# A one-core attention and mixing block: more idle products on TensorE, some of them into other PSUM sums, and a new instruction order

## The chip, the core and the metric

The kernel runs on one core of a Trainium2 chip. The metric is the device time of one execution in microseconds (us). Three executions of the kernel before took 656.92, 652.56 and 657.92 us, median 656.92. A core has TensorE (PE, with its weight loads PEld), VectorE (DVE), ScalarE (ACT), GpSimd (POOL) and SyncE (SP), which issues the DMAs; each runs its own instruction list strictly in the order in which the program gives it. A wait at the head of a list therefore holds everything behind it on that engine.

## The reference

```python
def _attn_ref(q, k, v, s):                       # q, k, v: (4, 8, 576, 64); s: (4, 8, 576)
    scores = scale * np.matmul(q, k.transpose(0, 1, 3, 2))
    cum = np.cumsum(np.maximum(s, 0.0), axis=-1)
    bias = -(cum[:, :, :, None] - cum[:, :, None, :])
    scores = np.where(causal, -1000000000.0, scores + np.minimum(bias, 0.0))
    attn = np.exp(scores - np.max(scores, axis=-1, keepdims=True))
    attn = attn / (np.sum(attn, axis=-1, keepdims=True) + 1e-09)
    return np.matmul(attn, v)
# x = heads side by side: (4, 576, 512)
#   h = relu(x^T @ w_tok1) @ w_tok2;  u = x + h^T;  u = u + relu(u @ w_ch1) @ w_ch2
#   out = (sigmoid(causal 5-tap convolution of u) * (u @ w_val)) @ w_out
```

## The kernel before

**Work.** The four batches run one behind the other, each in four pairs of heads. A pair `b_hp` loads q, k and v, scales and splits them, and goes through five query tiles i = 0 to 4: `score` (PE writes a PSUM bank `S`, DVE masks it into `x` with a running minimum), `expo` (ACT), the transposed probabilities, then `av` (PE multiplies them with v). All `av` products of a pair land in one PSUM bank, `xbank`: tiles 0 to 2 first, then `norm` and `x_value` read that bank (DVE, or DVE and ACT) and write `x32`, and only then may tiles 3 and 4 write the same columns. The four pairs of the first batch are "wide": their probabilities are transposed on PE (`p_turn`: tiles `p` and `pb`, copied out by ACT) and multiplied in 32-bit form. The later pairs split the probabilities in two 16-bit halves (`p_split`, tile `p`) and transpose them by DMA. Behind the pairs of a batch come token mixing (`t`), channel mixing (`c`, on `u` and `hT`), gate, `v` and `o`.

**Weights.** In the first 160 us the weights are decoded too. Each chunk of a weight is loaded (`raw`), unpacked by ACT and DVE into `arena`, and summed on PE: `dec.summed` adds products of a matrix of ones with the chunk to an open PSUM sum `ws_<name>`, in four steps of 128 columns for most chunks. The largest sum gives the weight's scale, by which ACT, POOL and DVE split it (`arena<-arena`).

**Order.** `ORDER` is a list of some 3,450 steps that a search wrote out: a letter for the engine (P, A, V, G, S) and a task's number. `Plan.run` takes the steps one by one and emits what they say; a replay of planned durations runs beside it. It decides one thing only: before each PE step `keep_warm` compares the planned time with how busy PE was planned to be, and where the share is under `WARM_FILL` it calls `plan.idle()`, which emits one product that nobody needs (an "idle product") so that the TensorE clock stays up. These products stand in PE's list for good. In the kernel before each writes columns 400 to 511 of `xbank` from a matrix of ones (line 530); there are 452. Because they write the bank that `norm` and `x_value` read, an idle product that stands behind those reads waits for them, and a read that stands behind an idle product waits for it.

Of the kernel before, what the change touches and what calls it, by code (L numbers as in the profile page):

```python
# [53 lines left out]
WARM_FROM, WARM_FILL, GAP1 = 12e3, 0.75, 13.87  # L54
# [27 lines left out]
S10 S0 V0 S7 P8 S12 A11 P1 V1 V1 A11 V11 P1 V1 V11 V1 P11 A9 A13 G4 A13 V13 V13 P13 S138 G6 S139 A9 G5 A3 G6 G6 S18  # L82
G6 A3 A2 V2 A2 G5 A141 A141 A141 S21 V9 V9 P9 V2 S2 S27 S32 V14 V14 A17 G17 P19 A20 A15 S140 S30 S191 V3 P142 V142
V142 P142 V142 V142 V142 A143 V143 A144 V144 S145 A20 V20 P28 A31 A31 V20 P20 S34 S145 V31 V31 P31 A33 A33 V33 V33
P33 G146 G16 S190 A22 A22 V22 V22 S46 P22 S41 S192 S44 A29 A29 V29 V29 V23 V23 G25 G25 G26 G16 A35 A35 V35 P29 S48
P149 P147 V147 A148 P155 V155 A156 P153 V153 A154 P169 V169 A170 V35 P157 A157 P175 V175 A193 S242 P171 V149 A150
P178 V178 P176 A193 P157 A157 A193 V171 A172 P179 V179 P161 P151 A151 V161 A162 P194 P159 V176 A177 V194 P157 A157
V194 P194 P173 A173 P35 V159 A160 A180 V194 V194 V194 V195 V195 G196 V196 S197 G24 S55 S197 V36 V36 V37 G37 S244
P152 G15 P42 P152 P158 P158 P163 A163 P173 A173 P163 A163 P181 A43 P173 P163 A163 P164 P164 V165 V165 V166 G167 A173
A45 A181 P181 A45 V45 A181 P181 P174 P174 V45 P45 A47 A43 V43 A181 P182 P182 S243 A47 V47 A49 V47 P47 A49 V49 A49  # L90
P168 A168 G167 V43 P43 V183 V183 V184 A185 G198 P199 P201 P211 P207 P230 P205 V199 P213 A200 V201 P221 A202 V211
P203 A212 V207 P227 A208 V230 A203 V213 A214 G49 P49 A245 S58 G185 P187 G24 P187 P215 V227 G39 V205 V221 P231 S69
S62 P223 A187 P228 P186 V40 G38 V187 P188 A245 S60 A215 P188 G188 A245 A206 V231 P246 V50 V228 P215 V50 P209 V246
P204 P204 V246 P246 V223 S294 V246 A222 V246 G39 V246 V248 V248 G247 V247 S249 S249 G250 G54 G54 A186 V189 V189 V189
G51 G51 P56 A209 P209 A215 A209 P209 A224 P225 A209 P210 A232 S296 A229 P215 A215 A59 P210 P233 A233 P216 P216 V217
V217 V218 G219 G219 A225 P225 A59 V59 V59 A57 A225 P233 A233 P225 A225 A57 V57 V57 P70 A71 P233 A233 A71 V71 V71
P226 P226 P234 P234 S295 P220 P57 A63 A63 V63 V235 A61 V63 V235 P71 S72 A61 A220 V61 A236 G237 G237 P251 V251 A252
P257 V257 A258 P265 V265 A266 P282 G53 P259 V259 A260 P59 P253 V253 A254 A297 A297 V61 P279 V279 P275 V275 G52 P273
P255 A255 V282 V273 P261 P61 S467 P63 V64 G40 P283 P263 A297 P298 V298 V298 G38 S74 A261 A73 P261 A261 V263 P298
V298 V298 V298 G300 S76 P280 A73 V283 V280 A264 A276 A274 V300 S468 P239 P239 A299 V299 S301 P267 A267 G302 A281  # L100
P261 A261 P267 P256 P256 P262 A239 P277 A267 A75 P267 P262 A277 P238 V64 G66 G66 G65 G68 A77 V73 V73 P73 S78 A267
S301 V239 P277 A75 V75 P268 P268 V269 V269 V75 A277 P277 A284 S469 P285 A238 V270 A77 A285 V77 P240 P240 G240 V241
V241 V241 G271 G271 P75 S80 P285 A470 A277 P278 P278 S525 A77 P272 A285 P285 A79 A79 V79 A272 P303 V303 P309 V309
A285 P327 V327 P317 P305 V305 P325 V79 V325 P311 V311 A470 G67 A310 G77 P77 S82 P286 G65 V317 A470 P471 V471 A304
P315 A328 G67 A306 P331 P307 V315 V471 V331 P286 V287 P471 V471 A81 V287 P334 G53 A326 A81 V81 A318 A312 P313 A307
A83 V288 G289 G289 V471 V81 P79 S84 V471 G473 P332 V332 P308 A313 A83 V83 A472 V472 P308 P81 S86 V473 S474 S474 P290
A290 A316 G52 G475 P329 V83 P313 A313 V334 A329 P291 P319 P313 A313 A319 P291 A291 V291 P329 P335 V335 P319 A85 A85
V85 P292 P292 G292 A319 P319 V85 G476 A329 P314 P314 V293 P83 S88 A333 A87 V293 V293 A319 P320 P320 V321 A87 A336
P337 A337 P337 A337 P85 S90 V87 V321 P329 V87 P87 P337 P477 P479 P484 V322 P491 G476 V323 V323 A329 P330 P330 P493
V479 P486 S92 V484 G68 S526 V477 A337 P338 P338 V491 P512 P509 A480 G476 S476 V482 V482 A478 V493 A89 G481 G481 S481  # L110
A485 V486 P502 G488 G488 A89 V89 V89 P89 A492 V339 V339 A91 A91 V91 S482 V509 A487 A340 G341 S108 V91 P504 A93 V341
S488 G489 G489 S527 P510 V510 A93 V93 S489 A528 P343 A494 A528 P343 A343 P324 V93 P93 V504 A108 A108 V343 P91 V94
G495 G495 V502 V94 V94 A324 A108 V108 P483 P483 S109 P342 A342 A503 P344 P344 A344 V345 A528 P529 V529 A95 G496 S495
V345 P110 G496 S496 V529 G506 G506 V345 P529 V512 A511 V346 S114 A515 P490 S506 V108 S112 P490 P346 V346 A111 V529
V346 A111 V111 A505 P346 V346 P513 G95 V529 V111 V529 G515 S515 A507 G507 A348 A350 V350 A349 V349 A530 V530 A531
# [346 lines left out]
def gated_block_kernel(  # L462
# [15 lines left out]
    nc = tc.nc  # L478
# [1301 lines left out]
```

## Time and profile before

| | us |
|---|---|
| median of three executions | 656.92 |
| the profiled execution | 659.9 |
| its span, first to last instruction | 658.1 |
| busy in the span: PE | 617.2 (94%) |
| DVE | 488.6 (74%) |
| ACT | 384.4 (58%) |
| POOL | 254.8 (39%) |
| mean granted TensorE clock | 0.979 |

The clock is a share of full speed: 1.00 is 2.4 GHz, 0.50 is 1.2 GHz, and those are its two levels; a figure between them is a mean over a stretch that has both. Busy PE is not PE at its peak, since a product lasts longer at the lower clock and the ends of products are modelled.

### The profile page before, as it was taken

Reading aid. Unit: us, or ns where it says so; the run is one execution under the profiler, and the core shown is the slowest. Engines: PE = TensorE matmul, PEld = TensorE weight load, DVE = VectorE, ACT = ScalarE, POOL = GpSimd, SP = SyncE. Lnnn points to the kernel's source line nnn. Section 1 sums busy time; section 2 is a strip of 40 time slices with the busy share of each in tenths; the row PEclk is TensorE's granted clock in tenths of the full one; section 3 lists DMA queues with packets and bytes.
Section 4 is the critical chain, followed back from the end, with each engine's and each line's share of the span. In section 5 each row is a group of like instructions: output and inputs, shape, how many; then the busy total and the mean of one; then the engine's idle time right before and its main releaser. Section 6 shows DMA issues by size and latency. Waiting matters only on the chain.

```text
span 658.1 us, 15930 instructions
## 1 busy us (share of the span) xinstructions
PE 617.2 (94%) x6059; PEld 498.4 (76%) x6059; DVE 488.6 (74%) x1380; ACT 384.4 (58%) x816; POOL 254.8 (39%) x367
## 2 busy tenths in 40 slices
PE   2899999969999979989998999999999999999997
PEld 2788888867778858767787887777877887678864
DVE  6888588887979968768687877877798943445672
ACT  5688498776768667645584655446576602204324
POOL 2457468343643432413454455713553210314000
PEclk9999599988999989999999999999999999999999
DMA  8986577686765828663747365844654400000002
GB/s 232 236 230 192 121 175 190 173 182 143 184 109 98 162 61 147 131 124 92 116 94 130 80 132 110 162 97 95 126 119 68 92 1 1 33 1 1 17 33 80
DMA packets 190806, 75.17 MB, mean 114 GB/s; under 512 B 178213, under 2 KB 181381, under 8 KB 190730
## 3 DMA queue, kind: packets, MB, share of 16 engines
q1 hardware_dynamic: 190730, 74.16, 51.3%
q8 instruction: 47, 0.77, 0.5%
q14 instruction: 29, 0.24, 0.1%
HBM read 33.89 MB, written 4.83 MB: 59 GB/s over the span
## 4 chain that ended last, share of the span: by engine, by line
PE 52%; DMA 4%; DVE 1%; ACT 1%; SPq 0%; issue 0%; POOL 0%; DVEq 0%; POOLq 0%; ACTq 0%
PE c L257 29%; PE o L257 7%; PE v L257 6%; PE t L257 3%; DMA pT<-p 3%; PE S L257 3%; PE xbank L257 3%; DMA qkT<-qk 1%; PE xT L257 1%; PE xm L257 1%; SPq L257 0%; DMA qk<-qkT 0%; ACT x L257 0%; DVE x L257 0%; DVE qk L257 0%
## 5 line engine op out<-in xcount | busy, mean ns | idle before, releaser
L257 PEld LDWEIGHTS <-arena 128*128 128x128 f16 x3168 | 288.9, 99 | 73.3 <-issue 4.1
L257 PE MATMUL c<-hT,arena 128*128 128x256 f16 (+1 forms) x1152 | 160.2, 287 | 3.6 <-DVE st L257 3.6
L257 PE MATMUL c<-u,arena 128*128 128x256 f16 (+1 forms) x1152 | 158.0, 288 | 0.0
L257 ACT ACTIVATE x<-x,st 128x448 f32<-128x448 f32 (+4 forms) x160 | 85.8, 556 | 56.9 <-DVE st L257 50.2
L257 POOL TENSOR_TENSOR p<-x,p 128x64 f16<-128x64 f32 (+4 forms) x83 | 68.7, 830 | 95.2 <-ACT p L257 72.1
L257 DVE CUSTOM_DVE_ANT_0 x<-S,mask,sc 128x64 f32<-128x64 f32 (+4 forms) x160 | 73.8, 485 | 25.1 <-PE S L257 13.5
L257 ACT ACTIVATE hT<-c 128x320 f16<-128x320 f32 (+1 forms) x96 | 36.3, 406 | 67.5 <-PE c L257 67.4
L257 PE MATMUL xbank<-v,pT 128*128 128x65 f16 (+1 forms) x880 | 64.9, 213 | 4.4 <-DMA pT<-p 3.3
L257 DVE SCALAR_TENSOR_TENSOR hT<-c,hT 128x320 f16<-128x320 f32 (+1 forms) x96 | 41.5, 449 | 27.8 <-ACT hT L257 27.6
L257 DVE SCALAR_TENSOR_TENSOR gate<-R,cwt,gate 128x320 f32<-128x320 f32 (+1 forms) x112 | 61.1, 564 | 1.2
L257 PE MATMUL S<-qk 67*128 67x288 f16 (+4 forms) x192 | 50.4, 285 | 4.1 <-DMA qk<-qkT 4.1
L257 PE MATMUL v<-x,arena 128*128 128x256 f16 (+1 forms) x384 | 53.9, 286 | 0.2 <-DVE x L257 0.2
L257 PE MATMUL S<-qkT 128*128 128x288 f16 (+4 forms) x192 | 50.5, 285 | 0.9 <-DVE st L257 0.9
L257 POOL TENSOR_SCALAR p<-x 128x192 f16<-128x192 f32 (+4 forms) x48 | 24.2, 505 | 61.5 <-ACT x L257 27.0
L257 PEld LDWEIGHTS <-pT 128*128 128x128 f16 x960 | 38.7, 98 | 9.4 <-DMA pT<-p 3.8
L257 PE MATMUL o<-arena,g 128*128 128x512 f16 x192 | 45.1, 379 | 0.0
L530 PE MATMUL xbank<-ones 128*128 128x112 bf16 x452 | 36.0, 228 | 6.4 <-DVE sums L257 2.9
L530 PEld LDWEIGHTS <-ones 128*128 128x128 bf16 x452 | 31.6, 108 | 9.4 <-issue 7.3
L257 ACT ACTIVATE gate<-gate 128x1280 f32<-128x1280 f32 (+1 forms) x24 | 27.9, 1162 | 14.4 <-DVE gate L257 14.0
L257 PEld LDWEIGHTS <-g 128*128 128x128 f16 x192 | 18.4, 98 | 18.1
L257 ACT ACTIVATE p<-x 128x576 f16<-128x576 f32 (+4 forms) x59 | 27.8, 477 | 5.8 <-DMA pT<-p 2.6
L257 DVE SCALAR_TENSOR_TENSOR qk<-stg,sg,qk 128x576 f16<-128x576 f32 x30 | 30.0, 1028 | 0.6 <-ACT qk L257 0.5
(209 smaller groups left out, 1090.6 us busy)
## 6 DMA issues: line engine op xcount, KB each, us to landing
raw<-in_moe_w_ch_dram SPq DMA_DIRECT2D x24, 512.0 KB, 4.6
stg<-in_q_dram SPq DMA_DIRECT2D x16, 288.0 KB, 3.3
stg<-in_k_dram SPq DMA_DIRECT2D x16, 288.0 KB, 5.3
qk<-qkT SPq DMA_DIRECT2D x32, 144.0 KB, 2.5
out_dram<-ot SPq DMA_DIRECT2D x16, 256.0 KB, 2.0
vst<-in_v_dram SPq DMA_DIRECT2D x24, 128.0 KB, 3.6
raw<-in_moe_w_val_dram SPq DMA_DIRECT2D x4, 512.0 KB
raw<-in_moe_w_out_dram SPq DMA_DIRECT2D x4, 512.0 KB
```

The lines of the kernel that those rows point to most:

```text
L257: return f(*a, **k)
L530: plan.idle = lambda: nc.tensor.matmul(xbank[:, 400:512], lhsT=ones, rhs=ones[:, 0:112], start=True, stop=True)
```

## The change

The share up to which PE is filled rises from 0.75 to 0.9. The idle product gets two forms. While nobody reads `xbank` (`read_x` is empty) it is as before. From the moment at which a `norm` has been emitted until the next `av` of tile 0 or 3 has been, it goes instead into the sum of a weight that is still open (`sums_w`): ones times columns of `mask` that hold zeros, added to that sum. If no weight's sum is open either, nothing is emitted, though the plan counts the time as filled. `ORDER` is a new list throughout; one line of each stands for it here.

```diff
-WARM_FROM, WARM_FILL, GAP1 = 12e3, 0.75, 13.87
+WARM_FROM, WARM_FILL, GAP1 = 12e3, 0.9, 13.87
...
-S10 S0 V0 S7 P8 S12 A11 P1 V1 V1 A11 V11 P1 V1 V11 V1 P11 A9 A13 G4 A13 V13 V13 P13 S138 G6 S139 A9 G5 A3 G6 G6 S18
...
+S0 V0 S7 S10 S12 S138 S139 S18 G4 P8 P1 V1 V1 P1 V1 V1 A11 A11 V11 V11 A13 G5 A13 V13 P11 A3 S21 G6 A3 V13 P13 A9 A2
...
     xbank = psX.tile([P, 512], F32, tag="X", name="xbank")
-    plan.idle = lambda: nc.tensor.matmul(xbank[:, 400:512], lhsT=ones, rhs=ones[:, 0:112], start=True, stop=True)
+    read_x, sums_w = [], []
+
+    def idle():
+        if not read_x:
+            nc.tensor.matmul(xbank[:, 400:512], lhsT=ones, rhs=ones[:, 0:112], start=True, stop=True)
+        elif sums_w:
+
+            ps, n = sums_w[-1]
+            for _ in range(max(1, 112 // n)):
+                nc.tensor.matmul(ps, lhsT=ones, rhs=mask[:, 0:n], start=False, stop=False)
+
+    plan.idle = idle
...
                 total = sum(ch[3] for ch in self.ch) * self.cw // self.nsum
+                if self.summed:
+                    sums_w.remove((self.ps, self.nsum))
                 for f in range(0, n, self.nsum):
...
                     self.summed += 1
+                if self.summed < total:
+                    sums_w.append((self.ps, self.nsum))
...
             if i in (0, 3):
                 yield PE, "X"
+                read_x.clear()
...
             xa = self.st["xa", h][:, 0:6 * DV].rearrange("p (i h d) -> p i h d", h=2, d=DV)
+            read_x.append(self)
```

The program holds 498 idle products after the change: 377 into `xbank` (line 534) and 121 into a weight's sum (line 539: 26 in `ws_c12`, 74 in `ws_c2`, 21 in `ws_wv`), against 452 into `xbank`. Ahead of the first score of the kernel there are 176 where there were 141.

PE's list in pair 0_1 (second pair of the first batch), from the last `av` of tile 2 to the first of tile 3, before; line 530 is the idle product, seven of them in the first gap, two in each of the two others:

```order
L257 MATMUL xbank_81<-v16_1_131,pT_0_1_2_1_1095 128x65 x2
L257 MATMUL xbank_81<-v16_1_131,pg_2_126 128x65
L257 MATMUL pb_0_1_3_0_1121<-ident_90,x_2_3_951 128x128 x3
L257 MATMUL pb_0_1_4_0_1132<-ident_90,x_2_4_946 128x128 x4
L530 LDWEIGHTS ones_79
L530 MATMUL xbank_81<-ones_79 128x112
...
L257 MATMUL pb_0_1_3_1_1146<-ident_90,x_3_3_1020 128x128 x3
...
L257 MATMUL pb_0_1_4_1_1160<-ident_90,x_3_4_892 128x128 x4
...
L257 MATMUL xbank_81<-v16_1_131,pT_0_1_3_0_1130 128x65 x3
```

The same place after the change:

```order
L256 MATMUL xbank_81<-v16_1_131,pT_0_1_2_1_1110 128x65 x2
L256 MATMUL xbank_81<-v16_1_131,pg_2_126 128x65
L256 MATMUL p0_0_1_4_1142<-ident_90,x_2_4_932 64x128
L256 MATMUL p0_0_1_4_1142<-ident_90,x_3_4_1004 64x128
L256 MATMUL pb_0_1_3_0_1154<-ident_90,x_2_3_963 128x128 x3
L256 MATMUL pb_0_1_4_0_1160<-ident_90,x_2_4_932 128x128 x4
L256 MATMUL pb_0_1_3_1_1165<-ident_90,x_3_3_1062 128x128 x3
L256 MATMUL pb_0_1_4_1_1173<-ident_90,x_3_4_1004 128x128 x4
L256 MATMUL xbank_81<-v16_1_131,pT_0_1_3_0_1158 128x65 x3
```

No idle product stands between tile 2 and tile 3 any more, and no weight's sum is open there: 16 transposes are all that PE has.

DVE's list at the same place, from the split of q and k (`qk16`) of the next pair to the value read (`x32<-xbank`) that frees `xbank`, before:

```order
L257 SCALAR_TENSOR_TENSOR qk16_0_2_1032<-stg_0_2_561,sg_0_2_996,qk16_0_2_1032 128x9x64 x2
L257 SCALAR_TENSOR_TENSOR R0_120<-t2_0_0_0_975,sg_0_0_253,R0_120 128x288
L257 SCALAR_TENSOR_TENSOR R0_120<-t2_0_0_1_986,sg_0_0_253,R0_120 128x288
L257 TENSOR_REDUCE amR0_122<-R0_120 128x1
L257 TENSOR_SCALAR sums_0_1_1114<-xbank_81,sc_0_1_586 128x6
L257 RECIPROCAL sums_0_1_1114<-sums_0_1_1114 128x6
L257 TENSOR_TENSOR x32_127<-xbank_81,sums_0_1_1114 128x384
```

And after:

```order
L256 SCALAR_TENSOR_TENSOR qk16_0_2_1079<-stg_0_2_563,sg_0_2_1041,qk16_0_2_1079 128x9x64 x2
L256 TENSOR_SCALAR arena_114<-arena_114,wsg_c10_716 128x512
L256 SCALAR_TENSOR_TENSOR R0_120<-t2_0_0_0_1012,sg_0_0_247,R0_120 128x288
L256 SCALAR_TENSOR_TENSOR R0_120<-t2_0_0_1_1020,sg_0_0_247,R0_120 128x288
L256 TENSOR_SCALAR sums_0_1_1145<-xbank_81,sc_0_1_613 128x6
L256 RECIPROCAL sums_0_1_1145<-sums_0_1_1145 128x6
L256 TENSOR_TENSOR x32_127<-xbank_81,sums_0_1_1145 128x384
L256 TENSOR_REDUCE amR0_122<-R0_120 128x1
```

The reduction `amR` has gone behind the value read, and one split of a weight (`arena`) has come ahead of it.

PE's list ahead of the first channel product `c1_0_0_0` of the kernel, before, from the last `av` of tile 2 of pair 1_0; nine idle products:

```order
L257 MATMUL xbank_81<-vsw_1_0_2028,pT_9_2_2253 128x65
L257 MATMUL cwT_2412<-ident_90,cst_2163 128x5 x4
L530 LDWEIGHTS ones_79
L530 MATMUL xbank_81<-ones_79 128x112
...
L257 LDWEIGHTS arena_114
L257 MATMUL c1_0_0_0_2434<-u16_0_0_2349,arena_114 128x320
```

And after, with 17 idle products, all into the sum of `wv`:

```order
L256 MATMUL xbank_81<-vsw_1_0_2013,pT_9_2_2262 128x65
L256 LDWEIGHTS qkT_1_0_1818
L256 MATMUL S_9_4_1_2430<-qkT_1_0_1818 128x288
...
L256 MATMUL ws_wv_2289<-raw_2153,ones_79 128x128
L256 MATMUL cwT_2460<-ident_90,cst_2207 128x5 x4
L539 LDWEIGHTS ones_79
L539 MATMUL ws_wv_2289<-mask_98,ones_79 128x128
...
L256 LDWEIGHTS arena_114
L256 MATMUL c1_0_0_0_2485<-u16_0_0_2425,arena_114 128x320
```

The products that wait for a reader of `xbank` have become products that wait for nobody; a score (`S_9_4_1`) and the last sums of a chunk have moved in ahead of them.

## Rows read from the trace of the kernel before

**Rows 1.** The span and mean granted clock of the core.

```profile
core 0: 658.1 us, clock 0.979
```

**Rows 2.** Busy time by stretches of 20 us; last: clock, DMA share, GB/s.

```profile
60.00:80.00 20.00, 17.27 (x122) 16.31 (x120) 12.75 (x26) 11.44 (x27) 10.40 (x13) 0.68 0.34 78
...
140.00:160.00 20.00, 17.08 (x155) 13.23 (x154) 16.33 (x38) 14.35 (x28) 6.03 (x7) 0.86 0.72 138
160.00:180.00 20.00, 20.00 (x197) 15.62 (x195) 18.78 (x47) 14.03 (x38) 11.95 (x18) 1.00 0.83 200
```

**Rows 3.** Timeline of PE in pair 0_1: start, us, instruction, [idle before <- releaser].

```profile
63.32 0.93 PE L257 MATMUL pb<-ident,x 128*128 128x128 f32 x7
66.41 0.50 PE L530 MATMUL xbank<-ones 128*128 128x112 bf16 x7 [2.16 <-DVE x L257]
...
68.35 1.50 PE L257 MATMUL xbank<-v,pT 128*128 128x65 f32 x6
...
76.34 0.84 PE L257 MATMUL xT<-ident,x 128*128 128x128 f32 x3
...
79.23 0.26 PE L257 MATMUL S<-qkT 128*128 128x64 f16 x1
```

**Rows 4.** Timeline of the other engines at the same place and ahead of it.

```profile
54.66 0.48 DVE L257 TENSOR_SCALAR arena<-arena,wsg_c 128x512 f16<-128x512 f32 x1
...
63.69 0.93 DVE L257 SCALAR_TENSOR_TENSOR R<-t,sg,R 128x288 f32<-128x288 f32 x2
...
64.66 0.75 DVE L257 TENSOR_REDUCE amR<-R 128x1 f32<-128x576 f32 x1
...
65.80 0.56 DVE L257 TENSOR_TENSOR x<-xbank,sums 128x384 f32<-128x384 f32 x1
...
68.42 1.11 SPq L257 DMA_DIRECT2D qk<-qkT  x2
...
76.58 0.22 DVE L257 TENSOR_SCALAR sums<-xbank,sc 128x4 f32<-128x4 f32 x1 [4.52 <-PE xbank L257]
```

**Rows 5.** The page's DMA issues: count, KB each, median us from issue to landing.

```profile
qk<-qkT SPq DMA_DIRECT2D x32, 144.0 KB, 2.5
```

**Rows 6.** Busy time by stretches of 3 us: PE, PEld, DVE, ACT, POOL, then clock.

```profile
63.00:66.00 3.00, 1.25 (x12) 1.08 (x12) 2.90 (x7) 2.09 (x5) 2.82 (x4) 1.00 0.35 67
...
72.00:75.00 3.00, 3.00 (x17) 3.00 (x16) 0.07 (x1) 0.26 (x1) 0.00 (x0) 0.50 0.02 5
...
84.00:87.00 3.00, 3.00 (x39) 2.80 (x37) 1.96 (x8) 1.88 (x5) 1.00 (x1) 0.98 0.30 66
```

**Rows 7.** Timeline of PE in pair 0_0: tile 3 and the next pair's first score.

```profile
45.06 0.78 PE L257 MATMUL xbank<-v,pT 128*128 128x65 f32 x6
...
50.88 0.19 PE L257 MATMUL S<-qkT 128*128 128x64 f16 x1
```

**Rows 8.** Timeline of PE at the first channel products.

```profile
147.69 0.60 PE L530 MATMUL xbank<-ones 128*128 128x112 bf16 x9 [2.92 <-DVE sums L257]
148.13 5.10 PE L257 MATMUL c<-u,arena 128*128 128x320 f16 x24
...
153.22 3.42 PE L257 MATMUL c<-u,arena 128*128 128x320 f16 x24
```

**Rows 9.** Timeline of DVE at the same place.

```profile
143.77 1.67 DVE L257 SCALAR_TENSOR_TENSOR u<-R,su,u 128x640 f16<-128x640 f32 x2
...
147.49 0.15 DVE L257 TENSOR_SCALAR sums<-xbank 128x6 f32<-128x6 f32 x1
```

**Rows 10.** Timeline of PE ahead of the first scores.

```profile
22.05 1.75 PE L530 MATMUL xbank<-ones 128*128 128x112 bf16 x32
...
29.71 0.19 PE L257 MATMUL S<-qk 67*128 67x64 f16 x1 [1.20 <-DMA qk<-qkT]
```

**Rows 11.** What PE waited for behind 150 us: us, times, longest.

```profile
PE c L257 <- DVE st L257: 3.6, 1, 3.6
```

**Rows 12.** Busy time by stretches of 3 us, as rows 6, behind that wait.

```profile
240.00:243.00 3.00, 1.96 (x11) 1.57 (x11) 2.19 (x8) 1.94 (x7) 0.40 (x1) 0.69 0.00 0
```

More of the change, by code (lines that the diff above doesn't have):

```diff
@@ L87 @@
[L87 to L91, printed above, removed]
@@ new lines @@
+P215 V50 P223 V230 P231 A187 V187 P188 V228 P188 G188 V205 P56 V231 A245 V50 G52 G51 A215 A245 P246 V246 V246 A206
+P209 P215 A229 P246 A222 A209 A215 P209 V223 A59 P204 P204 A209 S294 A224 G54 V246 V246 V246 G247 V248 V247 V248
+S249 S249 V37 G54 G53 P209 A209 A59 P215 A215 P225 A225 A232 S296 P210 V189 P70 A71 A71 V189 P210 P216 P216 P233
+V217 V217 V218 G219 A233 V189 V71 V71 P225 A225 P233 P225 A233 A225 P233 A233 P226 P226 P234 P234 G51 V59 V59 P59
+A57 A57 V57 V57 A63 A63 V63 P220 A61 V235 V235 A61 V63 A220 P71 G250 P251 A236 V251 A252 P253 V253 A254 P259 P257
@@ new lines @@
+P344 G495 G495 V504 A324 P344 P342 S489 G496 G496 S496 A528 V94 V512 A108 V108 G506 A342 S495 G344 V345 V345 P529
+V529 P110 G506 V345 A95 A111 S116 G95 P490 S506 A511 A515 V529 V346 V108 P346 V346 P529 V529 V346 A111 V111 A505
+P346 V346 S112 V529 G515 P490 P497 P497 V111 V529 A507 G507 S507 A348 A349 V349 A350 V350 P513 A530 V530 A96 V498
+P111 S114 A534 V96 V513 S515 A531 V531 S532 A97 V97 A113 V98 V98 V498 P108 A117 P351 P351 P353 P353 P355 P355 A354
+V354 P357 P357 A113 V113 V113 P113 P359 P359 A352 S583 A99 A533 A356 A499 P508 G534 V352 P361 P361 A514 P508 G534
@@ new lines @@
+P824 A1301 P1119 P1119 V1303 A832 P1255 V1113 V824 V825 V825 S1322 A815 A826 V826 A1304 P1120 P1253 P1233 P1095
+P1095 A1253 A1233 S1322 P1341 P1325 P1120 S1286 P1287 P1287 G1324 S1374 A1255 V1256 P1122 P1122 V1256 P1350 V1256
+P1123 G1296 G1296 V1325 P1327 G1297 S1296 V1096 P1334 V1288 V1288 G1297 V1350 P1360 S1297 A1305 A815 A1376 A1376
+A1376 P1377 G1324 V1289 P1298 P1298 S1324 V1121 P1291 A1326 V1377 V1377 P1377 G1305 V1327 P1097 P1097 A1328 P1123
+G1306 G1306 V1341 P1357 P1124 P1124 V1377 S1305 A1291 P1099 P1099 S1306 P1307 P1307 A1330 S1375 A1351 V1377 V1377
@@ new lines @@
+P1332 V1098 P1140 P1140 A1290 V1330 V1360 P1339 A1342 G1329 V1329 V1334 A1335 P1101 P1101 S1330 V1290 A1379 V1354
+S1329 V1344 V1344 A1098 V1098 V1100 P1361 S1344 A1337 A1382 V1332 A1333 V1308 V1308 A1309 P1331 P1331 V1379 V1337
+V1357 P1358 P1352 V1102 V1358 G1354 G1378 S1354 S815 A1310 G1310 P1312 P1311 P1312 V1339 P1142 P1142 V1361 A1336
+G1336 S1337 A1359 A1340 A1343 A1312 G1102 V1378 V1352 A1353 V1312 P1313 P1313 S1336 P1338 P1338 V1125 G833 A1141
+V1141 V1102 P1114 P1114 P1114 P1116 P1116 P1116 S1380 A1363 A1313 G1343 S1343 P1345 P1345 S1380 P1144 A1311 V1314
@@ L242 @@
+V1556 V1554 V1549 A1551 A1550 V1555 V1554 V1556 V1553 V1556 V1555 V1551 V1553 A1557 A1557 A1557 V1550 P1564 P1564
+P1566 P1566 P1568 P1568 S1480 A1500 A1482 P1570 P1570 S1482 A1573 P1562 P1562 A1573 S1573 A1561 S1561 A1563 S1563
+A1558 V1565 V1567 V1567 V1567 V1569 V1571 V1571 V1571 P1574 P1574 P1574 P1576 P1576 P1576 A1575 S1575 A1577 S1577
 """
```

289 lines of the change are left out of this document (135 added, 154 removed).

## The prediction

> **What bounds the kernel now.** The cores' view comes first: the span is 658.1 us at a mean granted clock of 0.979 [rows 1]. If the lost share were all at half speed, that is (1 - 0.979) x 658.1 = 13.8 us of PE's work, so the clock alone is worth about 2%. The stretches of 20 us say where: 0.68 in 60 to 80 us and 0.86 in 140 to 160 [rows 2], with smaller dips between and behind. From 160 us on PE shows 20.00 busy of 20 at clock 1.00 [rows 2], so what reaches that stretch earlier ends earlier, as long as PE stays the bound; DVE is at 18.78 of 20 there and is the next.
>
> The timeline of PE shows how the first dip arises [rows 3]. At 63.32 PE turns seven blocks of probabilities, until 64.25. Then seven idle products stand at the head of its list; they write `xbank` and wait 2.16 us, until 66.41, for the value read that DVE ends at 65.80 + 0.56 = 66.36 [rows 3, 4]. In 63 to 66 us PE is busy 1.25 of 3; then the clock goes to 0.50 and is back at 0.98 only in 84 to 87 [rows 6]. In 72 to 75 PE is busy all 3 us at 0.50 while DVE has 0.07, ACT 0.26 and POOL nothing [rows 6]: here everybody waits for a slow PE. DVE's next norm waits 4.52 us for the end of the `av` products, at 76.58 [rows 4]. The product that was to hold the clock is the one that lets it fall.
>
> The second place is the start of the channel products. DVE ends the second half of `u` at 143.77 + 1.67 = 145.44 [rows 9]. The first `c` product starts at 148.13, because nine idle products ahead of it waited 2.92 us, until 147.69, for DVE's read of `xbank` at 147.49 [rows 8, 9]. The first 24 products then take 5.10 us, a later run of 24 takes 3.42 [rows 8].
>
> **Pair 0_1, part by part.** The change takes the 11 idle products out from between tile 2 and tile 3. DVE's part keeps its place: `amR`, 0.75 us [rows 4], goes behind the value read, a split of 128x512 comes ahead of it, 0.48 us by the nearest one [rows 4]. So `xbank` is free at about 66.4 as before (0.3 us earlier by these two rows, which I leave out). PE now has two more transposes (`p0`) and the 14 of `pb` ahead of tile 3: at 0.93 / 7 = 0.13 us [rows 3] these 16 last 2.1 us and end near 65.5, and PE is then idle for 0.9 us instead of 2.16. Tile 3 starts at 66.4 instead of 68.35 [rows 3], 1.95 us earlier, whatever the clock does. If the clock stays up, the way from tile 3 to the next pair's first score goes as in pair 0_0: 50.88 - 45.06 = 5.8 us [rows 7], where it now takes 79.23 - 68.35 = 10.9 [rows 3]. The score then comes at 66.4 + 5.8 = 72.2. Its other input, the copy of `qk`, is issued by 68.42 + 1.11 = 69.5 and lands 2.5 us later, at 72.0 [rows 4, 5], so it doesn't decide. The gain is 79.2 - 72.2 = **7.0 us**, or 1.95 if the clock falls all the same. That DVE, ACT and POOL can follow is seen in 72 to 75, where they are nearly empty [rows 6].
>
> **The first channel products.** The 17 idle products ahead of them now add zeros to the open sum of `wv` and wait for no reader. `c1_0_0_0` can start when `u` is done, 145.5 instead of 148.13: 2.6 us. If PE no longer stands still for 2.92 us the clock should hold, and the first 24 products give back 5.10 - 3.42 = 1.7. That is 4.3 us on PE. But DVE, which must split the weights of the second channel product and trim every `hT`, is at 18.78 of 20 soon after [rows 2], and its list there is the same. Between nothing (DVE takes all of it) and 4.3 I take **3.0**, nearer the upper end, since PE at 20.00 is fuller than DVE.
>
> **What is added.** 46 more idle products, at 1.75 / 32 = 0.055 us each [rows 10], are 2.5 us if none is covered. Of the 35 more ahead of the first score (1.9 us), 1.20 lie in PE's wait for the `qk` copy [rows 10], which leaves 0.7. The others stand where DVE or ACT is late. I take **0.5**; the bounds are 0 and 2.5.
>
> **The new order behind 160 us.** SP's list keeps the same transfers in nearly the same order, and so does DVE's; neighbours change places. PE's largest wait there, 3.6 us for a score's bank to come free [rows 11], with the clock at 0.69 behind it [rows 12], costs 3.6 + (1 - 0.69) x 3 = 4.5 us; a piece of `c2` now stands ahead of the score at which it arose, so it can shrink. Another such wait can arise somewhere else. I take 0, with 4.5 either way as bounds.
>
> **The sum.** 7.0 + 3.0 - 0.5 = 9.5 us off the profiled execution, 659.9 us (span 658.1 and 1.8 around it): 650.4. That execution is 3.0 us above the median of the runs shown, 656.92, so against the median it is 656.92 - 9.5, or **647.5 us**. A measurement of this kernel can tell about 1%, 6.6 us, from no change.
>
> **Rivals.** (1) The clock falls in pair 0_1 all the same. For it: no idle product is left between tiles 2 and 3, since no sum is open there, and the 0.9 us of standing still follow transposes only. Against it: the wait is less than half as long. Then that term is 1.95 instead of 7.0, and the time is 656.92 - (1.95 + 3.0 - 0.5) = 652.5 us. The trace has no stretch of transposes alone, without idle products, by which to decide. The Trainium skill (TensorE: Matmul & The Clock Gate, Part 4: PE-mode transpose) says that work in transpose mode doesn't count as a busy PE in the same way and that the full clock doesn't engage for it; by that rule 652.5 would be the forecast, and no row here shows it.
>
> (2) The time gets longer through the new order: batches 1 to 3 are re-ordered throughout, and the chain transposed probabilities, `p` buffers, `x` buffers, score, bank can stall PE in more places as it does once now, for 3.6 us plus the clock, 4.5 in all [rows 11, 12]. Two more of these, with the 9.5 gained, give 656.92 - 9.5 + 9 = 656.4, no change; from three on it is slower (661 us), from four on by more than 1%. For it: the list was made by a search over planned durations, and the stall that is there now was planned away too. Against it: the order of the transfers is almost kept.
>
> (3) The new order also loses that stall: 647.5 - 4.5 = 643 us. (4) The change does not do what it says, because DVE bounds the stretch from 66 to 220 us: only the waits at 66 and 148 are moved, and it is 655 to 657. Against it stands DVE's 0.07 in 72 to 75 [rows 6].
>
> **Chances.** Forecast 0.45 (644 to 651 by itself), (1) 0.20, (2) 0.15, (3) 0.12, (4) 0.08. Faster by over 1% is below 650.3: most of the forecast (0.40), all of (3), and a fifth of (1): 0.56. Slower by over 1% is above 663.5: the worse half of (2) and a little for a mishap in the first 60 us: 0.10. The rest, 0.34, is within 1%. The range is 641 to 658 us: it leaves out the better end of (3) and the worse half of (2).
>
> **What the profile after would show.** Pair 0_1: no idle product that waits for DVE between tiles 2 and 3, a PE gap of under 1 us, clock 1.00 in 63 to 84 (0.50 means rival 1), the third pair's first score near 72 us. Start of `c`: within 0.3 us of the end of `u`, the first 24 products in about 3.4 us, all of it some 10 us earlier than 148. If the start of `c` has come forward by 9 us and the end has not, (2) or (4) holds: PE's waits behind 160 us have grown, or DVE's busy share has risen to the full. The forecast is wrong in its first step if PE waits in pair 0_1 for DVE as long as before, because something else holds DVE ahead of the value read.

## The result: 18.3 us on the first chip, 13.1 on another, against a forecast of 9.5

After the change the median is 636.89 us (636.05 to 637.18, four executions) beside 655.21 before (652.56 to 657.92, four): a ratio of 0.972 [0.967, 0.977]. On another chip it was 639.10 beside 652.20, 0.981 [0.978, 0.984] (`after_again`, below). The forecast was 647.5 us with a range of 641 to 658: the direction held, and the time lies below the range.

One thing must be known ahead of all readings: 69 further executions of the kernel before lie between 648.4 and 661.6 us and go with their mean granted clock (43 with 0.986 to 0.995, median 651.7; 26 with 0.973 to 0.984, median 657.6), and the profiled one [rows 1] is at the upper end. The kernel after has 0.999 or 1.000 in all four executions of the first chip, within 1.1 us.

| us | before | after |
|---|---|---|
| profiled execution, span | 659.9, 658.1 | 636.05, 634.3 |
| busy PE | 617.2 (94%) | 608.8 (96%) |
| DVE, ACT, POOL | 488.6, 384.4, 254.8 | 482.3, 385.4, 265.6 |
| clock | 0.979 | 0.999 |

The cores' view of the kernel after:

```profile
core 0: 634.3 us, clock 0.999
```

Busy time of PE, PEld, DVE, ACT, POOL, then clock, DMA share and GB/s, from the start to the first channel product and from there to the end; of before:

```profile
0.00:148.13 148.13, 122.20 (x1282) 111.26 (x1283) 118.64 (x365) 111.18 (x245) 78.04 (x113) 0.93 0.75 192
148.13:658.10 509.97, 495.01 (x4781) 387.17 (x4778) 369.94 (x1017) 273.18 (x572) 176.74 (x255) 0.99 0.45 92
```

and of after:

```profile
0.00:130.84 130.84, 116.85 (x1332) 107.13 (x1333) 112.65 (x354) 108.80 (x244) 77.32 (x113) 1.00 0.83 211
130.84:634.30 503.46, 491.91 (x4777) 385.52 (x4774) 369.64 (x1016) 276.61 (x581) 188.27 (x267) 1.00 0.47 94
```

17.3 of the 23.8 us between these two executions lie ahead of the first channel product, 6.5 behind it. In front PE's waits fell from 25.9 to 14.0 us (length minus busy), behind from 15.0 to 11.6; the rest is shorter busy time, with the clock at 0.93 against 1.00 in front and at 0.99 against 1.00 behind. The forecast had 9.5 in front and 0 behind.

The two places of the forecast, after. The timeline of PE in pair 0_1 [rows 3]:

```profile
61.15 0.93 PE L256 MATMUL pb<-ident,x 128*128 128x128 f32 x7
62.32 1.08 PE L256 MATMUL pb<-ident,x 128*128 128x128 f32 x7 [0.24 <-DVE R L256]
63.78 0.85 PE L256 MATMUL xbank<-v,pT 128*128 128x65 f32 x6 [0.38 <-DVE x L256]
...
69.46 0.19 PE L256 MATMUL S<-qkT 128*128 128x64 f16 x1
```

and the stretches that answer to [rows 2, 6, 12]:

```profile
60.00:80.00 20.00, 19.38 (x211) 17.80 (x211) 18.93 (x57) 17.93 (x42) 11.49 (x14) 1.00 0.73 174
140.00:160.00 20.00, 19.52 (x188) 14.73 (x185) 18.36 (x42) 15.30 (x37) 9.31 (x12) 1.00 0.71 172
...
72.00:75.00 3.00, 3.00 (x41) 2.67 (x39) 2.85 (x10) 2.94 (x10) 2.92 (x4) 1.00 1.20 286
240.00:243.00 3.00, 2.53 (x36) 1.80 (x35) 2.60 (x11) 1.46 (x4) 0.55 (x2) 1.00 1.06 217
```

PE waits 0.62 us in two pieces where it waited 2.16, the clock stays at 1.00, and in 72 to 75 us the other engines work instead of waiting for PE. The first channel products [rows 8]:

```profile
129.88 1.12 PE L539 MATMUL ws_wv<-mask,ones 128*128 128x128 bf16 x17
130.84 0.30 PE L256 MATMUL c<-u,arena 128*128 128x320 f16 x1
131.31 3.29 PE L256 MATMUL c<-u,arena 128*128 128x320 f16 x23 [0.17 <-DVE u L256]
...
134.60 1.79 PE L256 MATMUL c<-u,arena 128*128 128x320 f16 x12
...
138.38 1.79 PE L256 MATMUL c<-u,arena 128*128 128x320 f16 x12 [1.93 <-DVE hT L256]
140.01 0.62 PE L256 MATMUL ws_wv<-raw,ones 128*128 128x128 bf16 x4
140.45 1.81 PE L256 MATMUL c<-u,arena 128*128 128x320 f16 x12
```

The idle products wait for nobody, and `c` starts while `u` is still being written. But at 138.38 PE waits 1.93 us for DVE: what is gained at the start meets a DVE that is late. The 49th `c` product stands at 140.45; in before it stands at

```profile
156.52 1.79 PE L257 MATMUL c<-u,arena 128*128 128x320 f16 x12
```

so the lead there is 16.1 us, less than the 17.3 at the first product, and the other 7.7 of the 23.8 are gained behind it.

**What the new list changes beside the order.** Many tasks may run on more than one engine, and the letter of a step says on which one it does. The new list has other letters for 186 tasks; 76 of these split probabilities, and 13 stand ahead of the first channel product. DVE has 1,043 steps where it had 1,054, ACT 730 for 723, POOL 307 for 304. "The new order" below therefore means the order and the choice of engine together; no run parts them.

### The profile page after: what moved, and what is told of

Read it like the earlier page. It is cut to its first block, busy times and chain, and to the rows that moved or that the text cites. A ratio compares the mean times of both kernels' runs of the same rounds, so it can differ in the third digit from the quotient of the medians.

```text
span 634.3 us, 16063 instructions
## 1 busy us (share of the span) xinstructions
PE 608.8 (96%) x6105; PEld 492.6 (78%) x6105; DVE 482.3 (76%) x1369; ACT 385.4 (61%) x824; POOL 265.6 (42%) x380
## 4 chain that ended last, share of the span: by engine, by line
PE 75%; DMA 10%; DVE 8%; SPq 2%; issue 2%; POOL 2%; ACT 1%; POOLq 0%; DVEq 0%; ACTq 0%
PE c L256 38%; PE xbank L256 7%; PE o L256 7%; PE t L256 6%; PE S L256 6%; PE v L256 5%; DMA pT<-p 4%; DMA qkT<-qk 3%; SPq L256 2%; DVE arena L256 2%; DVE qk L256 1%; DMA qk<-qkT 1%; PE xT L256 1%; DVE x L256 1%; POOL p L256 1%
## 5 line engine op out<-in xcount | busy, mean ns | idle before, releaser
L256 ACT ACTIVATE x<-x,st 128x192 f32<-128x192 f32 (+4 forms) x160 | 85.8, 556 | 54.7 <-DVE st L256 50.9
L256 DVE CUSTOM_DVE_ANT_0 x<-S,mask,sc 128x192 f32<-128x192 f32 (+4 forms) x160 | 74.4, 485 | 23.3 <-PE S L256 18.1
L256 PE MATMUL xbank<-v,pT 128*128 128x65 f16 (+1 forms) x880 | 62.1, 208 | 2.3 <-DMA pT<-p 1.6
L256 DVE SCALAR_TENSOR_TENSOR gate<-R,cwt,gate 128x320 f32<-128x320 f32 (+1 forms) x104 | 58.1, 576 | 1.2
L256 PE MATMUL S<-qk 67*128 67x64 f16 (+4 forms) x192 | 49.2, 278 | 2.4 <-DMA qk<-qkT 2.4
L256 PE MATMUL S<-qkT 128*128 128x64 f16 (+4 forms) x192 | 49.2, 277 | 0.2
L256 ACT ACTIVATE p<-x 128x576 f16<-128x576 f32 (+4 forms) x66 | 31.6, 485 | 6.9 <-DMA pT<-p 4.4
L256 POOL TENSOR_SCALAR p<-x 128x320 f16<-128x320 f32 (+4 forms) x37 | 17.4, 469 | 36.2 <-DMA pT<-p 15.6
L256 PE MATMUL xbank<-vsw,pT 128*128 128x65 f16 x240 | 30.3, 194 | 0.0
L256 ACT ACTIVATE top<-raw 128x512 f32<-128x512 f32 (+2 forms) x36 | 22.5, 629 | 12.7 <-DMA raw<-in_moe_w_tok_dram 4.3
```

What stands on the lines that cost most here:

```text
L256: return f(*a, **k)
```

## The experiments

Each ratio is against executions of before on the same chip in the same round. The runs are spread over several chips, so edits of the kernel after are compared with it through these ratios and through the profiles.

### Order or idle products, front or back

Two kernels change one thing throughout: `order_alone` has the new list with before's idle product and fill, `idle_alone` the old list with the new idle function and 0.9. Two are spliced at the first step of `c1_0_0_0` (up to there both lists have done the same steps but one, some of them on other engines): `front_new` and `back_new`.

```diff
+        for ii, step in enumerate(ORDER.split()):
+            self.fill, self.idle = self.first if ii < 858 else self.later
...
+    plan.first, plan.later = (0.9, idle), (0.75, old)     # front_new; the reverse, at 859, in back_new
```

> The changed order throughout, with the idle products of before (all into xbank, fill 0.75). Theory 'idle products carry the gain': the idle products still stand at the head of PE's list in pair 0_1 and ahead of c1, so 7.0 + 3.0 of the 18.3 stay lost: 646 to 648 us, clock 0.50 for some 15 us behind 62 us. Theory 'order carries the gain': the reads of xbank come earlier in the new order, the idle products wait for little: 637 to 640 us.

> Before's order, with the new idle products and the fill of 0.9. Theory 'idle products carry the gain' (the prediction's terms 7.0 + 3.0 - 0.5 belong to them alone): 645 to 647 us, clock 1.00 in 63 to 84. Theory 'order carries the gain': 652 to 655, since with the old order PE still has nothing to do until DVE's value read at 66 us and the clock falls with or without idle products.

> The changed order and the changed idle products up to the first channel product c1_0_0_0 (step 857 of the list); from there the order, the fill of 0.75 and the idle products of before. Theory 'front and back' (from the two traces: c1_0_0_0 starts 17.3 us earlier, the profiled execution of before is 4.7 us above its own median, the pair at 250 us is still 15.7 earlier): the front alone is worth 12 to 14 us, so 641 to 643 us. Theory 'front only' (what was mis-sized is the front, the order behind it does nothing, as predicted): 18, so 637. Theory 'as predicted' (9.5 of the 18.3 come from the front, the rest from behind): 645.7.

> The reverse: before's order and idle products up to the first channel product, the changed ones from there. Theory 'front and back': the stall at 237 to 241 us and DVE's waits for idle products at 280 to 300 are gone, 4 to 6 us, so 649 to 651 us. Theory 'front only': no change, 655 +- 1. Theory 'as predicted': 8.8, so 646.4. If the two gains do not add up to 18.3, front and back share a wait.

Measured: `order_alone` 647.8 us, 0.988 [0.980, 0.995]; `idle_alone` 649.6, 0.994 [0.989, 0.998]; `front_new` 643.8, 0.982 [0.975, 0.990]; `back_new` 649.0, 0.988 [0.979, 0.997] of before. The gain is neither in one part nor in one half: by the ratios front 11.5 and back 7.9 (off 656.9) add up to 19.4, about the whole, though each interval is some 5 to 6 us wide to either side. Of the theories, "idle products carry the gain" fits `order_alone`; `idle_alone` lies between its two ranges, `front_new` 0.8 us above the range of "front and back", `back_new` at its lower edge. The forecast's 0 for the part behind falls here.

Two later runs take out every idle product, from after and from before:

```diff
-    plan.idle = idle
+    plan.idle = lambda: None
```

> The kernel after without any idle product (498 fewer). Theory 'the new order holds the clock by itself, since its PE never stands still for over 2 us behind 62 us': 636 to 640. Theory 'the idle products of the first 130 us hold it' (377 into xbank, most of them where PE waits for the decoded weights): the clock falls to 0.50 in several stretches ahead of 130 us, 645 to 660.

> The kernel before without any idle product. Old order with the old ones: 652 to 657; with the new ones 649.6. Theory 'the order is what gained': with none of them PE still stands still for 1.2 us in pair 0_1, some 2 us ahead of c1 and 4 us at 237, the clock falls at two or three of these places: 648 to 655, no clear difference to before. Theory 'the old idle products were the loss': 640 to 645.

`no_idle` 636.4 us, 0.976 [0.973, 0.980], beside 639.1 for the kernel after on the same chip: it isn't slower without them, rather 2.7 us faster (all four executions lie below all four of the kernel after). `before_no_idle` 643.4, 0.984 [0.980, 0.989]: 10 us gained by nothing but leaving out the products that were to hold the clock. So the second theory of its expectation came out. The timelines of all twenty traces, cut at the first `c` product, show what belongs to what:

| order, idle products | start of `c` (us) | from there to the end (us) |
|---|---|---|
| old, old (before) | 148.1 | 510.0 |
| old, new (`idle_alone`) | 135.3 | 511.9 |
| old, none (`before_no_idle`) | 133.1 | 510.3 |
| new front, old back (`front_new`) | 132.7 | 512.8 |
| old front, new back (`back_new`) | 144.1 | 506.3 |
| new, old (`order_alone`) | 141.7 | 502.4 |
| new, new (after; `after_again`) | 130.8; 133.3 | 503.5; 504.2 |
| new, none (`no_idle`) | 131.7 | 503.7 |

The start of `c` goes with the form of the idle product (139 to 148 in the eight traces where one waits for readers of `xbank` in pair 0_1 or ahead of `c` in the old list or, in the new one, in pair 0_1; 131 to 135 in the other twelve); the rest goes with the order: 508.6 to 514.7 in the eight traces with the old one behind `c` (at the low end `late_new`, below, which takes the new list from 264 us), 500.6 to 506.3 in the twelve with the new one. Where the two lists have the same idle products, the new one takes 7.6 us less behind the start of `c` with the old form, 8.4 or 7.7 with the new form and 6.6 with none.

`early_idle` and `late_idle` keep only the idle products ahead of step 378 (some 66 us), or only those behind it:

> The complement: only the idle products of the first 66 us. Theory 'early ones cost, late ones hold the clock': falls at 76 and 128 us as in no_idle, first t at 51.7, 638 to 642. Theory 'they do nothing at all': 636 to 639.

> The kernel after with the idle products only behind the last av step of pair 0_1 (step 378, some 66 us); those of the first 66 us are left out. Theory 'early ones cost, late ones hold the clock': first t at 50 to 51, no fall at 76 and 128 us, 633 to 636. Theory 'they do nothing at all': 636 to 639, as with all and with none.

640.6 us, 0.978 [0.974, 0.983], and 639.0, 0.978 [0.973, 0.982]: no difference between them. `late_idle` keeps the clock at 0.997 to 1.000, `early_idle` at 0.988 to 0.992, with the falls at 77 and 128 us that were expected; but the kept clock gains nothing that this measurement sees. My theory on early and late ones falls for the time. `fill75`, the kernel after with the old fill (411 idle products for 498), says the same of their number:

> The kernel after with the fill at 0.75 again: 87 idle products fewer (411 for 498), order and their new form as they are. Theory 'the number is not what holds the clock' (the prediction's cost of 0.5 us for 46 more): 636 to 637, clock 1.00. Theory 'more of them hold it': the clock falls once or twice, 640 to 643, and the runs spread.

638.9 us, 0.975 [0.968, 0.982].

### Pair 0_1

`gap_empty` takes only the 11 idle products of the gap out of the kernel before, `gap_old` puts the 12 that the replay wants there back into the kernel after:

```diff
-    plan.idle = lambda: nc.tensor.matmul(xbank[:, 400:512], ...)
+    plan.idle = lambda: None if 355 <= plan.at <= 381 else nc.tensor.matmul(xbank[:, 400:512], ...)
```

```diff
-        if not read_x:
+        if not read_x or 358 <= plan.at <= 374:
```

> The kernel before, with nothing taken out but the 11 idle products between tiles 2 and 3 of pair 0_1 (steps 355 to 381). The prediction's own first term alone: PE's wait there falls from 2.16 to about 0.9 us, the clock stays at 1.00 in 63 to 84 us, and the third pair's first score comes 7.0 us earlier than in the profile of before; in the time 5 to 7 us less, so 650 to 652 beside 656.9. Rival 'transposes do not hold the clock': the clock falls to 0.50 all the same, the score comes 1.95 us earlier, the time 1 to 2 us less. Rival 'the gain is given back at the first channel products, where DVE is late': the score comes early, but c1_0_0_0 within 2 us of where it was and the time with it.

> The mirror of the first: the kernel after, with the 12 idle products that the replay wants between tiles 2 and 3 of pair 0_1 put back into xbank. Theory 'the first term is right, and adds to everything else': PE waits some 2 us at their head, the clock falls to 0.50 in the 10 us behind, the third pair's first score comes 6 to 7 us later, the time is 642 to 644 beside 636.9. Rival 'what matters is the earlier value read in the new order, not the idle products': 637 to 638, clock 1.00.

`gap_old`: 643.0 us, 0.982 [0.972, 0.992] of before. That lies 4 to 6 us above the two medians of the kernel after, in the range of the first theory, but its four executions spread from 639.2 to 650.3 us and no execution of after was taken on that chip, so the time doesn't decide. The profile does: from the first `t` product of pair 0_0 to that of 0_1 it takes 35.4 us where after takes 27.8. PE's timeline in it, and the stretches behind:

```profile
63.86 0.36 PE L534 MATMUL xbank<-ones 128*128 128x112 bf16 x4 [2.27 <-DVE x L256]
```

```profile
66.00:69.00 3.00, 3.00 (x16) 3.00 (x15) 1.68 (x3) 2.35 (x5) 2.53 (x3) 0.50 0.44 101
69.00:72.00 3.00, 3.00 (x18) 3.00 (x18) 1.38 (x3) 1.58 (x3) 0.00 (x0) 0.50 0.01 3
```

`gap_empty` went against all that I had expected: 660.9 us, 1.010 [1.004, 1.015], the only edit that made the kernel before slower. Its timeline and stretches:

```profile
62.82 2.01 PE L257 MATMUL pb<-ident,x 128*128 128x128 f32 x14
66.00 0.85 PE L257 MATMUL xbank<-v,pT 128*128 128x65 f32 x6 [1.17 <-DVE x L257]
```

```profile
66.00:69.00 3.00, 3.00 (x21) 3.00 (x21) 2.93 (x5) 3.00 (x7) 2.83 (x4) 0.68 0.50 96
69.00:72.00 3.00, 3.00 (x16) 3.00 (x15) 1.39 (x3) 0.36 (x1) 0.27 (x1) 0.50 0.51 120
```

The wait is down to 1.17 us and the clock falls all the same. In `before_no_idle` the same 14 products and the same wait stand at the same place, and the clock holds:

```profile
63.97 2.00 PE L257 MATMUL pb<-ident,x 128*128 128x128 f32 x14
67.14 0.85 PE L257 MATMUL xbank<-v,pT 128*128 128x65 f32 x6 [1.17 <-DVE x L257]
```

```profile
66.00:69.00 3.00, 1.86 (x17) 1.89 (x17) 2.86 (x8) 3.00 (x7) 2.82 (x5) 1.00 0.92 177
69.00:72.00 3.00, 3.00 (x30) 2.99 (x29) 2.96 (x6) 1.84 (x4) 1.32 (x2) 1.00 0.47 112
```

So does it in `idle_alone`, again with 1.17 us. Over all traces: with idle products in this gap (a wait of 2.15 to 2.27 us) the clock fell in 7 of 7, without them in 1 of 13. Those 13 are not alike: in three, with the old list, PE waits 1.17 us in one piece, and one of the three lost the clock; in the ten with the new list it waits in two pieces, 0.62 to 1.36 us together, and none did. Why it fell in that one stays open, and so does why `gap_empty` is slower than before in its ten executions (clock 0.972 to 0.990). Its profile only says where: `c` starts at 144.4 us, 3.8 earlier than in before, but from there to the end it takes 514.8 us, the longest of all traces, with two waits of 2.4 us at 290 and 356 us that are 1.5 and 1.8 in before.

Does a wait of that size bring the clock down? `amr_back` puts DVE's `amR` back ahead of the value read in the kernel after (`V189` moved four steps up, no other change):

> The kernel after, with DVE's reduction amR (0.74 us) put back ahead of the value read in pair 0_1, as it stood before; every idle product at its place. The value read comes 0.7 us later, so PE's two waits among the transposes (0.24 + 0.38 us in the profile of after) grow to some 1.3 us. Theory 'near 1.2 us the clock may or may not fall' (it fell in the profile of gap_empty, with a wait of 1.17, and held in that of idle_alone, with the same wait): runs spread, some at clock 1.00 and 637.5 us, others at 0.98 to 0.99 and 640 to 643; the longest at least 2 us above the shortest. Theory 'the weight sums and other products around it hold the clock, whatever stands in the gap': all runs at clock 1.00, 636.9 to 638.

```profile
64.11 1.08 PE L252 MATMUL pb<-ident,x 128*128 128x128 f32 x7 [0.45 <-DVE R L252]
66.11 0.85 PE L252 MATMUL xbank<-v,pT 128*128 128x65 f32 x6 [0.91 <-DVE x L252]
```

The two waits grew to 1.36 us together, the clock was 0.995 to 1.000, the time 638.4 us, 0.975 [0.968, 0.982], within 0.9 us over four executions: my theory that this is the edge falls, at least for a wait in two pieces.

### The first channel products

`c1_idle` gives before's nine idle products there the new form, `c1_old` gives after's 17 the old one (both by the step's number, as above).

> The kernel before, with the nine idle products ahead of c1_0_0_0 put into the open sum of wv instead of xbank, nothing else. The prediction's second term alone: c1 starts within 0.3 us of the end of u instead of 2.7 behind it, the first 24 products take 3.4 us instead of 5.1, and 3.0 us are left at the end: 653 to 654 beside 656.9. Rival 'DVE bounds the stretch behind it': c1 starts earlier, a wait of PE for DVE behind it grows by as much, and the time is the same (656 to 657).

> The kernel after, with the 17 idle products ahead of c1_0_0_0 written into xbank instead of the sum of wv. Theory 'as in the prediction, 3.0 us at the end': PE waits some 2 to 3 us for the read of xbank, c1 starts 2.5 us later, the clock may fall behind it: 639 to 641. Theory 'DVE bounds the stretch from 138 us (PE's one longer wait of after, 1.93 us for hT, stands there) and takes it': 636.9 to 638.

`c1_idle`: 651.3 us, 0.998 [0.993, 1.003], too wide to tell 3.0 from nothing; in its profile `c` starts 0.5 us after the first of its idle products instead of behind a wait of 2.9 us, and the stage from the first `t` product of pair 0_3 to `c` is 14.7 us, where it is 16.5 to 18.8 in the five traces with the old list and the old form:

```profile
141.07 0.68 PE L534 MATMUL ws_wv<-mask,ones 128*128 128x128 bf16 x9
141.59 3.65 PE L251 MATMUL c<-u,arena 128*128 128x320 f16 x24
```

`c1_old` asks the same in the new order: 637.0 us, 0.973 [0.967, 0.979]. Its timeline:

```profile
132.82 1.75 PE L534 MATMUL xbank<-ones 128*128 128x112 bf16 x17 [2.30 <-DVE sums L256]
134.36 4.16 PE L256 MATMUL c<-u,arena 128*128 128x320 f16 x24
...
138.52 1.79 PE L256 MATMUL c<-u,arena 128*128 128x320 f16 x12
...
140.21 1.79 PE L256 MATMUL c<-u,arena 128*128 128x320 f16 x12
...
142.28 1.81 PE L256 MATMUL c<-u,arena 128*128 128x320 f16 x12
```

`c` starts 3.5 us later than in the kernel after and runs in part at half clock (4.16 us for 24): its 25th product comes 3.9 us later (138.52 beside 134.60). But the wait of 1.93 us for DVE's `hT` is gone, so the 37th comes only 1.8 us later (140.21 beside 138.38), from the 121st on it is 0.9 and at the end of the span 0.7 (635.0 beside 634.3). Most of what an earlier start gains is lost to DVE again, and the time shows no difference: in the new order the term is worth between nothing and 1 us.

### The first 50 us

`cum_first` gives before the first four steps of the new list (`S0 V0 S7 S10` for `S10 S0 V0 S7`: the load of the running sums ahead of the first weight's), with every idle product kept at its place; `cum_late` takes them back from after. `after_again` is the kernel after, on a second chip.

> The kernel before, with the first four steps of the new order (S0 V0 S7 S10: the running sums' load is issued ahead of the first weight's), every idle product of before kept at its place. Theory 'the early gain is this load': DVE's first wait falls from 3.8 to about 0.7 us, the first av-to-t step of pair 0_0 (53.5 us) comes 2 to 3.3 us earlier, and the time falls by 2 to 3 us, 654 to 655. Rival 'the weights are the bound of the first 50 us': the first weight's sums end later by the time of one load, some 1 us, and t stays within 1 us of 53.5: 656 to 658.

> The kernel after, with the first weight's load issued ahead of the running sums' again (S10 S0 V0 S7), every idle product at its place: the mirror of cum_first on a kernel whose runs lie within 1.1 us of each other. Theory 'this load is the early gain' (stage up to the first t 3.3 us shorter in the profile): t of pair 0_0 at 52 to 53 instead of 50.2, time 638.5 to 640. Theory 'most of the early gain is the order of the weights' decoding': less than 1 us, 637 to 638.

> The kernel after, unchanged, as the reference of this chip for its edits (amr_back 638.4, cum_late 639.0, c1_old 637.0, fill75 638.9). Theory 'the edits cost what was measured': 636 to 637.3. Theory 'it is the chip, and the first 50 us vary by 1 to 2 us': 637.5 to 639, with the first t at 51 to 52 us instead of 50.2.

`cum_first`: 650.2 us, 0.996 [0.992, 1.000]. DVE's first work on the sums, in its timeline, in `cum_first`:

```profile
2.73 0.64 DVE L252 TENSOR_SCALAR cum<-cum 32x576 f32<-32x576 f32 x1 [0.76 <-DMA cum<-in_s_dram]
```

and in before:

```profile
5.74 0.45 DVE L257 TENSOR_SCALAR cum<-cum 32x576 f32<-32x576 f32 x1 [3.77 <-DMA cum<-in_s_dram]
```

3 us earlier there, and the first `t` product of pair 0_0 starts at 51.7 instead of 53.5 (52.6 to 56.6 in four other traces that share this front). `cum_late` 639.0 us, 0.977 [0.970, 0.983], can't be told from `after_again`, 639.1: the mirror shows nothing. The first `t` of after is at 50.2 in one execution and 51.7 in the other, so this stage varies by as much as the edit moves, and what the load is worth stays open.

### Behind 160 us

`late_new` keeps before up to step 1624 (some 264 us) and takes the new list from there.

> Before's order and idle products up to step 1624 of the list (an output product of the second batch, some 264 us in the trace), the new order from there. From the first channel product to the end the traces with the old order take 509.6 to 514.7 us, those with the new one 502.4 to 506.3. Theory 'the stall at 237 to 241 us is the gain': this one takes 508 to 511, and the time is 653 to 656. Theory 'the gain is spread over the transfers of probabilities behind it': 505 to 507, and the time is 648 to 651.

652.5 us, 1.000 [0.996, 1.005], and 508.6 us from `c` to the end: the first theory, with a time 0.5 us under its range. So the gain behind `c` arises for the most part between `c` and 264 us, where the stall stands. PE's waits behind `c`, up to 330 us (us in total, times, longest), in `late_new`:

```profile
PE c L251 <- DVE st L251: 4.1, 1, 4.1
PE xbank L251 <- DMA pT<-p: 1.3, 2, 0.9
```

and in the kernel after:

```profile
PE c L256 <- DVE hT L256: 1.9, 1, 1.9
PE v L256 <- DVE st L256: 1.7, 1, 1.7
PE xbank L256 <- DMA pT<-p: 1.2, 2, 0.7
```

`c<-DVE st` [rows 11] is in all eight traces with the old list behind `c`, with 2.8 to 4.2 us, and in the twelve with the new one no such wait exceeds 0.5. What is late there is seen on DVE and POOL in before, at the wait that ends at 241.04:

```profile
240.43 0.55 DVE L257 CUSTOM_DVE_ANT_0 x<-S,mask,sc 128x320 f32<-128x320 f32 x1 [3.45 <-POOL p L257]
```

```profile
236.48 0.24 POOL L257 TENSOR_SCALAR p<-x 128x64 f16<-128x64 f32 x1 [2.59 <-DMA pT<-p]
237.70 0.57 POOL L257 TENSOR_SCALAR p<-x 128x448 f16<-128x448 f32 x1 [0.98 <-DMA pT<-p]
...
239.06 0.46 POOL L257 TENSOR_SCALAR p<-x 128x320 f16<-128x320 f32 x1 [0.43 <-DMA pT<-p]
239.61 0.79 POOL L257 TENSOR_TENSOR p<-x,p 128x320 f16<-128x320 f32 x1
```

DVE's mask of a score waits until 240.40 for POOL, which still reads the `x` that it wants to write, and POOL waited three times for the transposing DMA of probabilities: the chain of the second rival. That it is the `x` buffer is read from the names, and wasn't tested. The new list takes just these three copies away from POOL: steps 655, 681 and 669, in before `G655`, `G681` and `G669`, are `V655` (DVE), `A681` and `A669` (ACT) in after. Whether that or the order of the steps takes the stall away, no run shows.

## Why the prediction was wrong

**Pair 0_1 (7.0 us): right in the profile.** From the first `t` of pair 0_0 to that of 0_1 it is 27.8 us instead of 34.4, 6.5 less, with a wait under 1 us and clock 1.00, as written. But 7.0 was read from an execution in which the clock stayed low for long: summed over stretches of 2 us, (1 - clock) x 2 x 2 us, it is 17.1 us at half clock. Five traces have before's steps and idle products there: in `c1_idle` the dip is 13.7 us and the stage 32.8, but in `cum_first`, `late_new` and `back_new`, with the same wait of 2.15 us, the dip is 3.4 us and the stage 29.2 to 29.3 us, so there the term is 1.4. That 7.0 and 6.5 agree is luck in the choice of the profiled execution. What I credited to "no idle products" is confirmed by the profile of `gap_old`, and not by `gap_empty`.

**First rival.** The clock doesn't fall behind transposes alone as a rule: 12 of 13 traces held it, after's with 16 of them (of the three with one wait of 1.17 us behind 14 transposes, two). The Trainium skill (TensorE: Matmul & The Clock Gate, Part 4: PE-mode transpose) says that such work doesn't count as a busy PE in the same way; the forecast by it was 652.5. The traces here bear this out in one of 13.

**First channel products (3.0): size wrong.** `c1_old` measured 0 to 1 us in the new order, near the bound "nothing, DVE takes all of it". I chose near the upper end because PE was fuller than DVE in the 20 us behind; what counted was above all the one wait for `hT` that the earlier start ran into. That the start came 17.3 us earlier is not this term: the stage from the first `t` of pair 0_3 to `c` got shorter by 5.7, of which `c1_idle` shows 1.8 to 4.1 for the form of the idle products.

**What is added (-0.5): not contradicted, but the wrong question.** No run takes out just the 46 more; `fill75`, with 87 fewer, isn't faster (638.9 us). What the sum had nothing for is what all 498 do: `no_idle` is 2.7 us faster than after on the same chip. In the old order the new ones cost more, 649.6 us beside 643.4 without any; the two profiles show 3.7 of these 6.2, and the rest stays open. That the gain in front is bought by products which fill, as the change reads, is wrong: `before_no_idle` has 10 us without any. That this equals 7.0 + 3.0 is chance, since it takes out the idle products of all other places too.

**The new order behind 160 us (0): the step that failed.** It lost the stall of [rows 11, 12], the third rival, which I had priced at 4.5 us and given 0.12, and the stretch gained 6.5 us in the profile, 7.9 [1.7, 14.0] in `back_new`. The premise was wrong too: the prediction had only neighbours change places in DVE's list, but the new list gives steps of 186 tasks to other engines, the copies on the stalled chain among them. I weighed "a list made by a search can stall elsewhere" against it instead of looking where, and on which engine, the freeing of the `x` buffer stands in the new list. The stall by itself was priced at 4.5; what makes up the rest is not shown. The most that PE waits at one place behind 160 us in after is 1.7 us.

**The first 50 us:** no term of the sum but a loss; it was a gain of 3.3 us in the two profiles. The load of the running sums may be part of it (53.5 to 51.7 in `cum_first`); `cum_late` doesn't show it. The sum by what was measured in the profiles: 3.3 (first stage), 6.5 (pair 0_1), 1.8 (pairs 0_2 and 0_3), 5.7 (up to `c`), 6.5 behind, in all 23.8. Between the medians there are only 18.3 and 13.1, in part because the profiled execution of before has the long dip; with the short one pair 0_1 gives 1.4 for 6.5, and the sum is 18.7.

## What to carry to other kernels

A product that is to keep the clock up should not write to a place that somebody reads: it can then stand at the head of the list, wait, and make the pause in which the clock falls, as it did in 7 of 7 traces here. Before tuning such products, time the kernel with none of them; here that was worth 10 us in the old order, and in the new one, at 636.4 us the shortest median of all runs, nothing shows a need for them. And when a re-ordered list has one large stall fewer to show, price it in the sum: look for it in the new list by the buffer that it waits for, and compare the lists by engine as well as by order.

## What the runs showed of the hardware

**Waits and the clock.** All 36 dips between 55 and 620 us of the twenty traces follow a wait of PE. Of 29 waits of 2.0 us and more a dip followed 25, of 33 between 1.5 and 2.0 it followed 7, of 49 between 0.9 and 1.5 it followed 4. Most dips are short (3.4 us at half clock by the sum above, some up to 10.2); the longest, of 13.7 and 17.1, are all in pair 0_1, and nothing in their rows tells why these lasted.

**The granted clock doesn't show the start.** In `no_idle` PE was busy 0.55 to 1.52 of every 4 us from 4 to 28 us; the column says 1.00 throughout, because the trace has no record of the clock ahead of 34 us there and the view counts that as full; but its first scores of 448 columns take 0.58 us, where after, with idle products ahead of them, takes 0.35. In `no_idle`:

```profile
29.66 0.58 PE L256 MATMUL S<-qkT 128*128 128x448 f16 x1
30.04 0.58 PE L256 MATMUL S<-qk 67*128 67x448 f16 x1
```

```profile
28.00:32.00 4.00, 3.80 (x18) 2.24 (x18) 2.67 (x12) 2.09 (x7) 3.73 (x5) 1.00 1.10 323
```

and in after:

```profile
29.23 0.35 PE L256 MATMUL S<-qkT 128*128 128x448 f16 x1
29.42 0.35 PE L256 MATMUL S<-qk 67*128 67x448 f16 x1
```

Even so the first `t` of `no_idle` comes at 50.5 us, not later than with the idle products (50.2 and 51.7): in the first 50 us PE isn't the bound.
